# Dropping a kernel's closing barrier, and moving one small variance operation forward, in a linear-attention plus gated-MLP layer

## The chip, the cores and the metric

The kernel runs on one core of one Trainium2 chip. The metric is the device time of one execution in microseconds. The time is a little longer than the span of the profile, which runs from the kernel's first instruction to its last. In this text PE is TensorE, DVE is VectorE, ACT is ScalarE, POOL is GpSimd and SP is SyncE, as in the profile.

Ratios are the mean time of one kernel's fast runs over the mean of the other's fast runs of the same rounds, so they are not quite the ratio of the medians that are quoted beside them.

## The reference

The input has 2048 tokens of 640 columns. It is normalised, and the result goes through a linear attention with 32 heads of 20 and through a gated MLP of width 1536; both are added to the input.

```python
def _layernorm(x, axis=-1, eps=1e-5):
    m = jnp.mean(x, axis=axis, keepdims=True)
    v = jnp.var(x, axis=axis, keepdims=True)
    return (x - m) / jnp.sqrt(v + eps)
# ... (in reference():)
    xn = _layernorm(x, axis=-1)
    return x + _A_ref(xn, A_wqkv, A_w_phi, A_wo) + _B_ref(xn, B_w1, B_w3, B_w2)
```

## The kernel before

The kernel records all operations as Python objects, orders them with a list scheduler, and then plays one list of waits and operations into each engine. Tokens are worked on in 16 tiles of 128. What matters here is the head, in which the first tiles are normalised so that PE can start, and the tail.

Tile 0 is normalised by DVE statistics and a POOL power of -0.5. The sums of tile 1 are made by ACT; two small DVE operations turn them into mean square and variance, and POOL makes `rstd` of it, the factor 1 / sqrt(variance) by which normalisation multiplies (`mv` holds mean and variance, `bst` DVE's statistics, `x_tok` the tokens):

```python
    def act_rstd(t):
        v, r = mv[:, t, 1:2], rstd[:, t, 0:1]
        small(v, sums[:, 0:1], sums[:, 8:9], ALU.subtract)          # DVE, 1 column
        P.op("POOL", "tensor_tensor", [r], [v, mhalf[:, 0:1]], (r, v, mhalf[:, 0:1], ALU.pow), cost=0.6)

    def ln_apply(t, lo=0, hi=D):      # (x - mean) * rstd on DVE for the first four tiles
        ...
    def norms():
        ...
        yield lambda: act_sums(1)
        yield lambda: ln_stats(0, 1)
        yield lambda: ln_sums(2, 0)
        yield lambda: act_mean(1)
        yield lambda: ln_apply(0, 0, 256)
        done["first"] = 1
        yield lambda: ln_apply(0, 256, D)
        done["first"], done["ln"] = 2, 1
        yield lambda: act_rstd(1)
        yield lambda: (ln_sums(2, 1), ln_rstd(2, 1))
        yield lambda: ln_apply(1)
        done["ln"] = 2
        yield lambda: ln_apply(2)
        ...
```

PE transposes each normalised tile and multiplies it with the V weights, which arrive in three pieces:

```python
    def first_loads():
        load_x(0, 1)                                    # SP's queue
        o = P.dma("ACT", x_tok[:, 1:2, :], x_t[:, 1:2, :])
        ...
        load_x(2, 3)
        for a, b in ((0, 2), (2, 4), (4, DC)):          # V weights
            P.dma("SP", WVK[:, a:b, 0:D], wqkv_t[:, a:b, 2 * D:3 * D])
        load_x(3, 4)
        ...
```

At the end SP waits for all output stores. The lists are played inside a block, and the block closes with a branch, a drain and an all-engine barrier. In the instruction records each engine's drain raises a semaphore; POOL waits for it (the gather) and then raises a second one (the release), for which the other four wait (265.648 to 265.864 us in the kernel before; the records are listed below):

```python
        for o in finish:
            lists["SP"].append(("wait", o.sem[2], o.sem[1]))
    ...
    with nc.allow_low_precision(...), nc.allow_non_contiguous_dma(...), nc.Block() as block:

        @block.sync
        def _(e):
            play(lists["SP"], nc.sync)
        # ... the same for tensor, scalar, vector, gpsimd
```

The softmax here doesn't subtract the row's maximum and nothing guards it: scores larger than these inputs give would overflow.

## Time and profile before

| | us |
|---|---|
| time, median of the first 3 runs (267.52 to 267.91) | 267.78 |
| span of the profiled run, whose time was 267.64 | 265.864 |
| SP's wait for the last store ends | 265.431 |
| time minus span | 1.78 |

The table of stretches of the kernel before; the numbers behind the engines are busy microseconds, with instructions in brackets, then the granted clock of PE.

```profile
core 0: us, PE busy (x) PEld busy (x) DVE busy (x) ACT busy (x) POOL busy (x), PEclk, DMA share, GB/s
0.00:7.11 7.11, 5.67 (x24) 2.47 (x24) 3.63 (x13) 3.88 (x8) 3.40 (x15) 1.00 0.69 218
7.11:263.57 256.46, 256.44 (x1867) 153.40 (x1867) 179.93 (x299) 102.42 (x218) 92.51 (x93) 1.00 0.44 101
263.57:265.90 2.33, 0.00 (x0) 0.00 (x0) 0.29 (x1) 0.00 (x0) 0.00 (x0) 1.00 0.23 70
```

Between 7.11 and 263.57 us PE has no free time, so only the head and the tail can give anything back without less work for PE. The chain of waits of the kernel before (start, length, what) shows the head's steps:

```profile
4.57 0.58 POOL rstd L104
...
5.43 0.37 DVE x_tok L104
5.81 0.12 DVE mv L104
5.93 0.41 DVE bst L104
...
6.36 0.22 DVE mv L104
...
6.61 0.46 DVE x_tok L104
7.07 0.05 issue
7.11 256.46 PE PS L104 x1867
263.57 0.02 issue
263.60 0.29 DVE xres L104
```

From 5.17 on, the chain is DVE alone: both pieces of tile 0, the variance of tile 1 (`mv`, 5.81), statistics of tile 2 (`bst`, `mv`), then tile 1 (`x_tok`, 6.61). The timeline of DVE and of POOL in the same kernel has the durations that the change shifts:

```profile
5.72 0.21 DVE L104 TENSOR_SCALAR mv<-sums 128x1 f32<-128x1 f32 x1
5.85 0.48 DVE L104 BATCH_NORM_STATS2 bst<-x_tok 128x6 f32<-128x320 bf16 x1
6.36 0.22 DVE L104 BATCH_NORM_AGGREGATE mv<-bst 128x2 f32<-128x15 f32 x1
6.61 0.45 DVE L104 TENSOR_SCALAR x_tok<-x_tok,mv,rstd 128x640 bf16<-128x640 bf16 x1
7.25 0.45 DVE L104 TENSOR_SCALAR x_tok<-x_tok,mv,rstd 128x640 bf16<-128x640 bf16 x1 [0.19 <-POOL rstd L104]
...
6.01 1.20 POOL L104 TENSOR_TENSOR rstd<-mv,mhalf 128x1 f32<-128x1 f32 x2 [0.87 <-DVE mv L104]
```

POOL's two powers (tile 1 at 6.01, tile 2 at 6.665) took 0.565 and 0.549 us in the instruction records; the first ends just when DVE is through with the aggregation.

The tail, from the instruction records of the trace (start and end in us, sequencer instructions included):

```
263.597 263.889  DVE   last addition
264.249          SP    last store issued (end of the issue)
265.403 265.431  SP    wait for the last store
265.471 265.512  SP    compare-and-branch
265.648 265.655  SP    drain
265.681 265.698  POOL  gather     265.759 265.776  POOL  release
265.801 265.864  SP, ACT, DVE, PE: wait for the release
```

### The profile page before, as it was taken

The page shows a single profiled execution, that of the slowest core. Times are in us where ns is not written, and L with a number is a line of the kernel's source. Part 1 is how long each engine was busy: PE and PEld are TensorE (multiplying, and loading weights), DVE is VectorE, ACT ScalarE, POOL GpSimd, SP SyncE. Part 2 cuts the span into 40 slices and gives each one's busy share as a digit, 9 for nine tenths or more (in the row PEclk, how much of TensorE's full clock was granted, in tenths as well). Part 3 has the DMA queues.
Part 4 walks back from the last instruction along what each step waited for, and adds up shares of the span by engine and source line. Part 5 has one row for each costly group of instructions (what it writes and reads, how often), then busy time and mean ns, then how long its engine had stood idle before and what let it go on. Part 6 is the DMA issues. An engine that isn't in the chain of part 4 may idle for free.

```text
span 265.9 us, 4695 instructions
## 1 busy us (share of the span) xinstructions
PE 262.1 (99%) x1891; PEld 155.9 (59%) x1891; DVE 183.9 (69%) x313; ACT 106.3 (40%) x226; POOL 95.9 (36%) x107
## 2 busy tenths in 40 slices
PE   7999999999999999999999999999999999999996
PEld 3655545565558556465565756455656564777773
DVE  4668999999796679696685858788769567512112
ACT  5546988699760452251405240263143322000000
POOL 4221587989997035106030523007303321000000
DMA  6997088723301981932525070613260626141211
GB/s 211 270 307 205 8 161 242 162 52 55 117 2 22 270 195 39 140 56 62 94 49 128 2 159 25 131 25 75 62 133 22 132 52 128 27 123 52 87 39 49
DMA packets 62742, 27.73 MB, mean 104 GB/s; under 512 B 49920, under 2 KB 62720, under 8 KB 62720
## 3 DMA queue, kind: packets, MB, share of 16 engines
q1 hardware_dynamic: 62576, 27.26, 44.0%
q8 instruction: 15, 0.25, 0.4%
q10 hardware_dynamic: 144, 0.16, 0.2%
q14 instruction: 7, 0.06, 0.1%
HBM read 12.81 MB, written 2.62 MB: 58 GB/s over the span
## 4 chain that ended last, share of the span: by engine, by line
PE 96%; DVE 1%; DMA 1%; POOL 0%; issue 0%
PE PS L104 96%; DMA x_tok<-in_A_x_dram 1%; DVE bst L104 1%; DVE x_tok L104 0%; DVE mv L104 0%; POOL rstd L104 0%; DVE xres L104 0%
## 5 line engine op out<-in xcount | busy, mean ns | idle before, releaser
L104 PE MATMUL PS<-xnT,w_s 128*128 128x512 bf16 x480 | 108.2, 379 | 0.0
L104 PEld LDWEIGHTS PS<-xnT,w_s 128*128 128x128 bf16 x480 | 46.4, 98 | 50.9
L104 POOL TENSOR_TENSOR eqt<-eqt,rS 128x600 bf16<-128x600 bf16 (+1 forms) x32 | 41.0, 1306 | 97.4 <-DVE rS L104 97.4
L104 ACT ACTIVATE th<-PS 128x512 f32<-128x512 f32 x48 | 28.6, 596 | 79.0 <-PE PS L104 78.9
L104 PE MATMUL PS<-w_s,hT 128*128 128x320 bf16 (+2 forms) x384 | 54.9, 299 | 0.0
L104 DVE SCALAR_TENSOR_TENSOR t<-th,PS 128x512 bf16<-128x512 f32 x48 | 32.4, 675 | 31.4 <-ACT th L104 31.4
L104 PEld LDWEIGHTS PS<-w_s,hT 128*128 128x128 bf16 x384 | 37.1, 98 | 15.1
L104 PE MATMUL PS<-WVK,xnT 128*128 128x512 bf16 (+3 forms) x260 | 45.6, 330 | 0.1
L104 POOL TENSOR_TENSOR ekt<-ekt,rS 128x640 bf16<-128x640 bf16 x32 | 39.8, 1276 | 4.8 <-DVE rS L104 4.8
L104 ACT ACTIVATE eqt<-PS 128x240 bf16<-128x240 f32 (+1 forms) x96 | 27.2, 348 | 25.9 <-PE PS L104 24.1
L104 DVE TENSOR_TENSOR xres<-PS,xres 128x640 bf16<-128x640 f32 (+2 forms) x17 | 13.3, 782 | 33.5 <-PE PS L104 33.5
L104 PEld LDWEIGHTS PS<-WVK,xnT 128*128 128x128 bf16 x260 | 24.2, 98 | 19.4 <-ACT WVK L104 0.4
L104 DVE SCALAR_TENSOR_TENSOR hT<-t,PS 128x512 bf16<-128x512 bf16 x48 | 33.0, 687 | 1.7
L104 DVE TENSOR_REDUCE S<-ekt 128x64 f32<-128x1280 bf16 x16 | 23.3, 1455 | 2.2 <-ACT ekt L104 2.1
L104 PE MATMUL PS<-wo_s,oT 128*128 128x320 bf16 (+2 forms) x160 | 24.5, 299 | 0.0
L104 PE MATMUL PS<-Wqp,xnT 128*128 128x360 bf16 (+1 forms) x160 | 24.3, 299 | 0.0
L104 DVE TENSOR_REDUCE S<-eqt 128x66 f32<-128x1320 bf16 x16 | 24.2, 1510 | 0.0
L104 ACT ACTIVATE ekt<-PS 128x640 bf16<-128x640 f32 x32 | 22.3, 703 | 1.3 <-PE PS L104 0.8
L104 PEld LDWEIGHTS PS<-Wqp,xnT 128*128 128x128 bf16 x160 | 15.2, 98 | 7.6
L104 DVE RECIPROCAL rS<-S 128x64 f32<-128x64 f32 (+1 forms) x32 | 17.9, 560 | 1.1
L104 PEld LDWEIGHTS PS<-wo_s,oT 128*128 128x128 bf16 x160 | 15.2, 98 | 5.9
L104 DVE TENSOR_TENSOR o_tok<-PS,g_s 128x360 bf16<-128x360 f32 (+1 forms) x32 | 15.7, 491 | 1.1
(50 smaller groups left out, 124.3 us busy)
## 6 DMA issues: line engine op xcount, KB each, us to landing
w_s<-in_B_w_dram SPq DMA_DIRECT2D x6, 640.0 KB, 6.4
xres<-in_A_x_dram SPq DMA_DIRECT2D x16, 160.0 KB, 2.5
out_dram<-xres SPq DMA_DIRECT2D x15, 160.0 KB, 1.9
x_tok<-in_A_x_dram SPq DMA_DIRECT2D x3, 640.0 KB, 4.8
w_s<-in_B_w_dram SPq DMA_DIRECT2D x1, 1920.0 KB, 9.3
wo_s<-in_A_wo_dram SPq DMA_DIRECT2D x1, 800.0 KB, 4.8
WVK<-in_A_wqkv_dram SPq DMA_DIRECT2D x2, 320.0 KB, 4.5
x_tok<-in_A_x_dram SPq DMA_DIRECT2D x3, 160.0 KB, 2.7
```

What stands on the lines that cost most here:

```text
L104: o = _Op(eng, lambda: m(*args, **kw), r, w, cost)
```

## The change

Intent: give back the 0.43 us that the block's close takes after the last store, and let POOL start on tile 1's `rstd` earlier by placing the variance between the two pieces of tile 0's normalisation.

```diff
         yield lambda: ln_apply(0, 0, 256)
         done["first"] = 1
+        yield lambda: act_rstd(1)
         yield lambda: ln_apply(0, 256, D)
         done["first"], done["ln"] = 2, 1
-        yield lambda: act_rstd(1)
         yield lambda: (ln_sums(2, 1), ln_rstd(2, 1))
@@
-    with nc.allow_low_precision(...), nc.allow_non_contiguous_dma(...), nc.Block() as block:
-        @block.sync
-        def _(e):
-            play(lists["SP"], nc.sync)
-        (... and so for the four other engines)
+    with nc.allow_low_precision(...), nc.allow_non_contiguous_dma(...):
+        for e in ("SP", "PE", "ACT", "DVE", "POOL"):
+            play(lists[e], P.eng[e])
```

The programs differ in nothing else: no matmul, no load and no other wait changes place on any engine. The barrier at the kernel's entry stays.

More of the change, by code (lines that the diff above doesn't have):

```diff
@@ L933, in play @@
                     r.then_inc(it[2], it[3])
-    with nc.allow_low_precision(reason="bf16 results"), nc.allow_non_contiguous_dma(reason="w_phi rows"), nc.Block() as block:
-        @block.sync
-        def _(e):
-            play(lists["SP"], nc.sync)
-        @block.tensor
-        def _(e):
-            play(lists["PE"], nc.tensor)
-        @block.scalar
-        def _(e):
-            play(lists["ACT"], nc.scalar)
-        @block.vector
-        def _(e):
-            play(lists["DVE"], nc.vector)
-        @block.gpsimd
-        def _(e):
-            play(lists["POOL"], nc.gpsimd)
+    with nc.allow_low_precision(reason="bf16 results"), nc.allow_non_contiguous_dma(reason="w_phi rows"):
+        for e in ("SP", "PE", "ACT", "DVE", "POOL"):
+            play(lists[e], P.eng[e])
 _INS = ['A_x', 'A_wqkv', 'A_w_phi', 'A_wo', 'B_x', 'B_w1', 'B_w3', 'B_w2']
```

## The prediction

> **What bounds the kernel now.** TensorE does. In the table of stretches it is busy 256.44 of the 256.46 us between 7.11 and 263.57 us, at granted clock 1.00. The chain of waits is 7.1 us of head, 256.46 us of PE, 0.29 us of the last VectorE addition; then the output store lands and the kernel closes. Only head and tail are left, and the change touches exactly these.
>
> **Tail (no block).** From the trace's instruction records, sequencer instructions included: SP's wait for the last store ends at 265.431. Then come SP's branch (265.471 to 265.512), SP's drain (265.648), POOL's gather and release (265.681 to 265.776) and every engine's release wait, the last (PE) ending at 265.864, which is the span. The instruction order of the changed kernel has neither these drains nor this barrier; its last instruction is SP's wait. That removes 265.864 - 265.431 = 0.43 us, all on the critical path, as nothing runs beside it.
>
> The time (267.8) is longer than the span. [...] The trace's semaphore records agree: nine updates of one semaphore, 277.400 to 277.931 on the trace's clock, 0.24 to 0.77 us after the span's end. Its third step comes 0.21 us after the second; the same step in the next such barrier takes 0.04. So some engine comes late there. Without the closing barrier four engines reach it well before SP, so this 0.17 us may vanish from the time too. Estimate for the time: -0.43 to -0.65 us.
>
> At the start each engine loses a branch. The trace shows none of these (the only branch recorded is SP's last), and the entry barrier stays. I expect 0 to 0.05 us.
>
> **Head (variance of tile 1 earlier).** In the timeline VectorE does: first piece (5.173), second piece (5.434), the small variance operation (5.723, taking a slot of 0.124), half statistics of tile 2 (5.847), aggregation (6.364 to 6.586), tile 1's normalisation (6.610 to 7.057). The last waits for POOL's rstd, whose semaphore comes at 6.585. After: the variance at about 5.434, the second piece at 5.558, the statistics unchanged, rstd done 0.29 earlier. VectorE then flows from the aggregation into tile 1 with its usual overlap of 0.08, starting near 6.50: 0.1 us earlier, not 0.29, because VectorE itself is the next limit. PE idles 0.225 before tile 1's transposes, so these come about 0.1 earlier. Tile 0's second transposes come 0.12 later, but PE waits for ScalarE's first copy then (6.34), so that hides. Tile 2's rstd doesn't move (it waits for the aggregation), so PE will now wait about 0.04 for it: net 0.06 us gained, carried through the saturated PE stream to the end.
>
> **Sum.** Span -0.5 us, to 265.4; time -0.5 to -0.7 us: 267.2 us, range 266.8 to 267.6. Chances: faster by over 2% 0.005, within 2% 0.99, slower 0.005.
>
> **What would show each step right or wrong.** Tail: the last instruction is SP's store wait, about 1.54 us after the last addition ends (before 1.98). Runtime: time minus span shrinks from 1.78 to about 1.6 or stays. Head: tile 1's normalisation starts near 6.50 without a wait for POOL, its transposes near 7.00, and the long PE piece starts or ends 0.05 to 0.1 earlier while its length stays near 256.4.
>
> **What would make it wrong.** The runtime's barrier may cost the same or take over the wait, leaving the time gain near 0.1; the second piece's delay of 0.12 may reach PE through ScalarE's second copy (6.242 to 6.734), eating the head's gain; a chip other than the one of before may differ by more than the effect.

(The figures "277.400 to 277.931 on the trace's clock" are 266.103 to 266.634 us from the span's start. These nine updates are called the barrier after the kernel below. "The runtime's barrier" stays as a name only, since no trace shows whose updates they are. -0.43 for the block's close, 0 to -0.17 for the nine updates, 0 to -0.05 for the start and -0.06 for the head come to -0.5 to -0.7, so 267.2. The 0 to 0.05 is the author's estimate; the one branch recorded, SP's last, takes 0.041. The "usual overlap of 0.08" is in the trace before: the small variance operation ends at 5.930, the statistics after it start at 5.847.)

## The result

| | before | changed |
|---|---|---|
| time, median of 6 runs | 267.68 (267.52 to 268.33) | 266.97 (266.52 to 267.33) |
| ratio of the fast runs, 95% interval | | 0.9968 (0.9953 to 0.9984) |
| time of the profiled run | 267.64 | 266.57 |
| its span | 265.864 | 265.337 |

This is within 2%, and the median is inside the predicted range. The parts of the sum are not all as predicted. The profiled pair can be taken apart completely. Both traces end with two bursts of nine updates of semaphore 2, which no instruction of the kernel names; the second runs from 267.464 to 267.821 in the kernel before and from 266.405 to 266.761 in the changed one. The first burst is the barrier after the kernel; that its steps wait for the engines is shown below. The time is 0.18 to 0.19 us less than the very last update in both traces (267.821 and 267.64; 266.761 and 266.57), and 0.18 to 0.20 less in all fourteen traces. So the measured time moves with the last update, and what makes these bursts end earlier makes it shorter.

| from the traces, us | before | changed | difference |
|---|---|---|---|
| SP's wait for the last store ends | 265.431 | 265.337 | -0.094 |
| from there to the last instruction (branch, drain, barrier) | 0.433 | 0 | -0.433 |
| from there to the first burst complete (the barrier after the kernel) | 0.770 | 0.278 | -0.492 |
| from there to the last update of the second | 1.187 | 1.146 | -0.041 |
| sum | 267.821 | 266.761 | -1.060 |

The third row is the surprise, and it is larger than the block's own closing barrier. The nine updates of the barrier after the kernel, in us from the span's start:

```
before   266.103 266.137 266.348 266.393 266.416 266.513 266.552 266.588 266.634   (kernel ends 265.864)
changed  263.642 263.676 263.715 263.945 265.451 265.496 265.534 265.568 265.615   (kernel ends 265.337)
```

In the changed kernel four of the nine updates are done long before SP ends. The stretches and the chain of the changed kernel, against those shown of before:

```profile
7.11:263.57 256.46, 256.36 (x1867) 153.15 (x1865) 180.08 (x300) 102.36 (x218) 92.63 (x93) 1.00 0.45 102
263.57:265.90 2.33, 0.00 (x0) 0.00 (x0) 0.23 (x1) 0.00 (x0) 0.00 (x0) 1.00 0.23 70
```

```profile
4.58 0.58 POOL rstd L104
...
5.44 0.21 DVE mv L104
5.65 0.30 DVE x_tok L104
...
5.99 0.34 PE PS L104 x3
6.34 0.01 issue
6.35 257.13 PE PS L104 x1871
263.48 0.02 issue
263.50 0.29 DVE xres L104
```

The last addition starts 0.1 us earlier (263.50, before 263.60). DVE's chain now ends with tile 0's second piece, and PE's unbroken part starts already at 6.35. The timeline of DVE and POOL in the changed kernel:

```profile
5.44 0.21 DVE L104 TENSOR_SCALAR mv<-sums 128x1 f32<-128x1 f32 x1
5.57 0.37 DVE L104 TENSOR_SCALAR x_tok<-x_tok,mv,rstd 128x384 bf16<-128x384 bf16 x1
6.51 0.38 DVE L104 TENSOR_SCALAR x_tok<-x_tok,mv,rstd 128x640 bf16<-128x640 bf16 x1
7.34 0.45 DVE L104 TENSOR_SCALAR x_tok<-x_tok,mv,rstd 128x640 bf16<-128x640 bf16 x1 [0.44 <-POOL rstd L104]
...
5.73 0.63 POOL L104 TENSOR_TENSOR rstd<-mv,mhalf 128x1 f32<-128x1 f32 x1 [0.58 <-DVE mv L104]
6.68 0.63 POOL L104 TENSOR_TENSOR rstd<-mv,mhalf 128x1 f32<-128x1 f32 x1 [0.32 <-DVE mv L104]
```

Tile 1 is normalised at 6.51 without a wait for POOL, as predicted; but both powers now take 0.63, so that tile 2 starts at 7.34 and not at 7.25. PE's timeline in the kernel before and, in the second fence, in the changed one:

```profile
6.34 0.72 PE L104 MATMUL PS<-WVK,xnT 128*128 128x320 bf16 x4
7.11 0.45 PE L104 MATMUL PS<-ident,x_tok 128*128 128x128 bf16 x5
7.40 0.71 PE L104 MATMUL PS<-WVK,xnT 128*128 128x320 bf16 x4
```

```profile
6.35 0.72 PE L104 MATMUL PS<-WVK,xnT 128*128 128x320 bf16 x4
6.96 0.45 PE L104 MATMUL PS<-ident,x_tok 128*128 128x128 bf16 x5
7.24 0.71 PE L104 MATMUL PS<-WVK,xnT 128*128 128x320 bf16 x4
```

PE comes to the second piece of the V weights (the last line of each) 0.16 us earlier; after tile 2's wait 0.09 of it is left at the end.

### The profile page after: what moved, and what is told of

Same layout as the page of the kernel before. It is cut to its first block, busy times and chain, and to the rows that moved or that the text cites. A ratio compares the mean times of both kernels' runs of the same rounds, so it can differ in the third digit from the quotient of the medians.

```text
span 265.3 us, 4684 instructions
## 1 busy us (share of the span) xinstructions
PE 262.1 (99%) x1891; PEld 155.8 (59%) x1891; DVE 183.8 (69%) x313; ACT 106.3 (40%) x226; POOL 96.1 (36%) x107
## 4 chain that ended last, share of the span: by engine, by line
PE 97%; DMA 1%; DVE 1%; POOL 0%; issue 0%
PE PS L104 97%; DMA x_tok<-in_A_x_dram 1%; DVE bst L104 0%; POOL rstd L104 0%; DVE mv L104 0%; DVE x_tok L104 0%; DVE xres L104 0%
## 5 line engine op out<-in xcount | busy, mean ns | idle before, releaser
L104 POOL TENSOR_TENSOR eqt<-eqt,rS 128x600 bf16<-128x600 bf16 (+1 forms) x32 | 41.1, 1307 | 97.3 <-DVE rS L104 97.3
```

The source lines that it names most:

```text
L104: o = _Op(eng, lambda: m(*args, **kw), r, w, cost)
```

## The experiments

Twelve further kernels ran, two of them the changed kernel again, all with correct results. The first four ran on one chip with 11 runs of the kernel before (median 267.71, 267.55 to 269.58), then four on a second chip, then four on a third with 11 runs of before (median 267.75, 267.35 to 268.32). Five rounds give 6 runs of each kernel.

| kernel | mean (lowest to highest) | time minus span, mean (range) | ratio to before, 95% interval |
|---|---|---|---|
| changed, first | 266.93 (266.52 to 267.33) | 1.25 (1.22 to 1.30) | 0.9968 (0.9953 to 0.9984) |
| no_block_only | 266.89 (266.61 to 267.13) | 1.22 (1.21 to 1.24) | 0.9960 (0.9940 to 0.9981) |
| variance_only | 267.95 (267.46 to 268.26) | 1.75 (1.71 to 1.78) | 1.0000 (0.9978 to 1.0021) |
| changed_again | 266.97 (266.49 to 267.64) | 1.25 (1.21 to 1.29) | 0.9963 (0.9939 to 0.9987) |
| barrier_back | 267.52 (267.27 to 267.73) | 1.73 (1.67 to 1.76) | 0.9986 (0.9964 to 1.0008) |
| v_weights_sooner | 267.55 (267.02 to 268.82) | 1.23 (1.19 to 1.27) | 0.9988 (0.9968 to 1.0008) |
| v_sooner_old_variance | 268.31 (267.15 to 269.93) | 1.24 (1.21 to 1.27) | 1.0016 (0.9986 to 1.0047) |
| changed_third | 266.84 (266.49 to 267.15) | 1.24 (1.19 to 1.27) | 0.9960 (0.9946 to 0.9974) |
| v_weights_later | 268.68 (267.22 to 269.61) | 1.23 (1.19 to 1.31) | 1.0031 (1.0001 to 1.0060) |

(Spans of single runs are listed to 0.1 us, so a single difference is good to about 0.05.) The 22 runs of before have a time minus span of 1.68 to 1.81. So this difference goes with a kernel's close, and the spread between runs of one kernel (0.46 to 2.78 us in this table) lies inside the span.

### Each half of the change alone

`no_block_only` is the changed kernel with the variance in its old place; `variance_only` is the kernel before with only the variance moved; `changed_again` is the changed kernel once more.

```diff
 no_block_only, against the changed kernel:
-        yield lambda: act_rstd(1)
         yield lambda: ln_apply(0, 256, D)
         done["first"], done["ln"] = 2, 1
+        yield lambda: act_rstd(1)

 variance_only, against the kernel before: the reverse of this, the block stays
```

> Only the block is removed; the variance keeps its old place. Theory (the time gain is the tail: 0.43 us of closing barrier plus about 0.49 us by which the runtime's own barrier after the kernel gets shorter; the head gives only 0.09): time 0.9 us below before (about 266.9), trace: last store's wait ends near 265.43 as before, the span ends with it, tile 1's normalisation starts near 6.61 as before, time minus span near 1.23. Rival A (the runtime's barrier costs the same, so the tail is worth only 0.43 and the rest is the head or drift between runs): about 267.3, time minus span near 1.78. Rival B (the head's reordering gives most): 267.5 or more.

> Only the variance is moved; the block stays. Theory: trace as in the changed kernel at the head (tile 1's normalisation near 6.51, tile 2's near 7.34, long PE part ends about 0.09 us earlier), tail as before (last store's wait to span's end 0.43, time minus span 1.78): time 0.1 us below before, which repeats can't tell from zero. Rival B (the head gives most of the 0.85 us): 0.5 us or more below before, clear of the interval.

> The changed kernel again, beside the others on one chip. Theory: 266.9 us, ratio 0.9965 to 0.997, head and tail as in its first trace; the single runs spread over 0.8 us as before, with time minus span near 1.23 in each, so that the spread lies within the span. Rival C (its first trace was a lucky fast run): a trace whose span is 265.8 or more, with a longer stretch somewhere that shows what the spread is.

Taking the block away alone gives all of the time that can be measured: its mean is 0.90 below the nine runs of before that stay under 269 us (mean 267.79; two runs were at 269.5), against 0.92 from the two rows of the tail (0.433 + 0.492), and time minus span is 1.22. (With the two runs at 269.5 in, the mean of before is 268.11 and the difference 1.22; their time minus span is as in the others, so they are long within the span. No trace shows why.) Its trace has the last store's wait end at 265.375 with the span, tile 1 at 6.564 and the barrier after the kernel complete 0.272 later. That decides against rival A (267.3, 1.78) and rival B.

Moving the variance alone shows nothing in the time (ratio 1.0000). Its trace has the head as in the changed kernel (tile 1 at 6.438, tile 2 at 7.263) and the tail as before (0.438 and 0.769). But the end of PE's work did not come 0.09 earlier: it came at 264.149, and in the trace of `changed_again` at 264.535, 1.07 later than in the changed kernel's first trace. That trace is the one that rival C named, with a span of 266.4. So the question was what makes a span longer by up to 1 us with the very same instructions.

The waits of `changed_again` between 5 and 10 us (engine, line, waited for: us in total, times, longest) answer it:

```profile
DVE bst L104 <- DMA x_tok<-in_A_x_dram: 1.3, 1, 1.3
PEld PS L104 <- ACT xnT L104: 1.3, 2, 1.0
PE PS L104 <- DMA WVK<-in_A_wqkv_dram: 0.9, 1, 0.9
```

PE waits for the second piece of the V weights. (The second line is the same wait, put down to the semaphore that the profile saw last: ACT's copies were over by 8.05.) Landing of that piece, PE's start on it, and end of PE's work, in all traces but that of `v_weights_later`, which comes below, in us:

```
                       landed   PE starts   PE ends   ends - starts
before                 7.039    7.404       263.559   256.16
changed                6.927    7.244       263.465   256.22
no_block_only          7.120    7.357       263.512   256.16
variance_only          7.727    7.863       264.149   256.29
changed_again          8.160    8.295       264.535   256.24
barrier_back           7.060    7.206       263.427   256.22
last_wait_on_pe        6.980    7.152       263.373   256.22
last_wait_on_dve       6.851    7.241       263.502   256.26
last_wait_on_pool      7.476    7.612       263.827   256.22
last_wait_on_act       7.075    7.448       263.605   256.16
changed_third          7.503    7.638       263.909   256.27
v_weights_sooner       6.523    7.695       263.917   256.22
v_sooner_old_variance  7.189    7.987       264.141   256.15
```

From its start on this piece PE needs 256.15 to 256.29 us in each of these traces. Where the piece lands at 7.47 or later, PE starts 0.135 to 0.136 after the landing, in all four such traces. So in the traces with the same order of loads the spans differ mainly through one load. (There is a second, smaller source: in `last_wait_on_act` the clock record has full clock only from 6.84 us on, the first matmuls on the V weights are 0.24 and 0.22 us apart instead of 0.136, and PE reached the second piece at 7.448 though it had landed at 7.075.) Of the load queue's packets that end between 3.5 and 8.5 us, the median one takes 0.055 us, but in `changed_again` 19 of 1257 take over 0.3 and the longest 1.54. The landing semaphore of a piece is raised in sixteen steps, and the table has the last of them: in `changed_again` fifteen steps were in by 7.105 and the sixteenth came at 8.160, where in the first trace of the changed kernel they end at 6.867 and 6.927. So one late step out of sixteen held PE up. That trace too has 17 of 1307 packets over 0.3 (longest 1.05), so their number does not tell the two apart. What makes single packets slow is not shown, nor which of them delayed that step.

### The barrier put back without the block

```diff
         for e in ("SP", "PE", "ACT", "DVE", "POOL"):
             play(lists[e], P.eng[e])
+        nc.all_engine_barrier()
```

> The changed kernel with one explicit all-engine barrier at its end: no block, no branches, but the barrier is back. Theory: the barrier alone is the cost. After SP's last wait some 0.25 to 0.30 us of drain, gather and release follow (0.43 before, less SP's branch and the 0.14 us after it), and the runtime's barrier becomes as long as before (time minus span 1.78): time 267.6 to 267.7, at most 0.25 below before. Rival D (the branches, or the block's placing of the instructions, were the cost): stays near 266.9.

In the trace, 0.265 us of drain, gather and release follow SP's last wait (265.290 to 265.555), and the barrier after the kernel again needs 0.769 from the end; time minus span is back at 1.73. The mean is 0.55 above `changed_again` on the same chip. The trace's parts, 0.265 + 0.49 = 0.76, would have it at 0.76; the runs' spread (0.46 and 1.15 us from lowest to highest) is wide enough for the difference. Rival D (the time stays near 266.9) falls: the barrier is most of the cost, 0.76 of the 0.92. Of the 0.433 us before, the other 0.17 went with SP's branch and the time until the drain behind it.

### Which engine ends last

Another engine than SP waits for the output stores:

```diff
         for o in finish:
-            lists["SP"].append(("wait", o.sem[2], o.sem[1]))
+            lists["PE"].append(("wait", o.sem[2], o.sem[1]))      # or DVE, POOL, ACT
```

> The changed kernel, but TensorE instead of SP waits for the output stores, so TensorE is the last engine to end. Theory (the engines reach the runtime's barrier one after another in a fixed order, with TensorE first and SP at the turn, so an engine that ends early takes its step early and only the steps from the last engine on remain): from the end of the last wait to the barrier's ninth update 0.55 to 0.62 us, against 0.278 with SP last; all nine updates come after that end. Rival (the barrier just starts later; which engine ends last makes no difference): 0.28 as with SP.

> The same with VectorE waiting for the stores. Theory (VectorE takes the fourth step: in the changed kernel the fourth update came 0.15 us after VectorE's last addition): three updates come long before the end, six after it, and the ninth 0.38 to 0.45 us after the last wait's end. Rival: 0.28.

> The same with POOL waiting for the stores. Theory (POOL takes the third step, and is the engine that came 0.17 us late in the kernel before): two updates before the end, the third 0.5 to 0.6 us after it, the ninth 0.8 to 0.9 us after it, the worst place of the five. Rival 1 (POOL takes the second step, ScalarE was the late one): one update before the end, the ninth about 0.6 us after it. Rival 2 (no order): 0.28.

> The same with ScalarE waiting for the stores. Theory (ScalarE takes the second step): one update before the end, the ninth 0.5 to 0.6 us after it. Rival (ScalarE is third and late): two updates before the end, the ninth 0.8 us or more after it.

Measured, from the end of the last wait, which is the span's end:

| waits last | updates before the end | end to its own first update | end to the ninth update |
|---|---|---|---|
| PE | 0 | 0.187 | 0.542 |
| ACT | 1 | 0.110 | 0.434 |
| POOL | 2 | 0.532 | 0.814 |
| DVE | 3 | 0.141 | 0.383 |
| SP (changed kernel) | 4 | 0.114 | 0.278 |
| all at once (kernel before) | 0 | 0.24 (PE's) | 0.770 |

Each place is one trace, but the counts are as the theory has them in all four: PE, ACT, POOL, DVE, SP take the steps of the barrier after the kernel in this order. The sizes were a little below what was expected for PE (0.55 to 0.62) and ACT (0.5 to 0.6), and within it for DVE and POOL. POOL alone comes 0.53 us after its last instruction, the others 0.11 to 0.19. This explains the row of before: the closing barrier lets all engines go at once, POOL's release ends at 265.776, and the third update comes 0.572 later, at 266.348; six more steps follow. Without the closing barrier POOL has taken its step by 263.715. So the 0.49 us are the steps of four engines, and above all POOL's, done while the last store was still on its way. Why POOL needs 0.53 is open.

### The V weights' landing moved, both ways

The orders of all compute engines stay exactly as in the changed kernel; only one load changes its place in a queue after the schedule is made.

```diff
 v_weights_sooner: the load of token tile 2 moves from SP's list to ACT's, behind that of tile 1
+    for it in [it for it in lists["SP"] if it[0] == "op" and it[1] is moved[-1]]:
+        lists["SP"].remove(it)
+        at = next(n for n, i in enumerate(lists["ACT"]) if i[0] == "op") + 1
+        lists["ACT"].insert(at, it)
 v_sooner_old_variance: the same, on no_block_only
 changed_third: no edit
 v_weights_later: the load of token tile 3 moves ahead of the V weights in SP's list
+    lists["SP"].insert(2, lists["SP"].pop(5))
```

> The changed kernel; only the load of token tile 2 is issued by ScalarE's queue behind that of tile 1 instead of by SP, so that SP issues the three pieces of the V weights 0.45 us sooner. Every compute engine's order is unchanged. Theory (the spread of 0.8 us between runs of one kernel is the landing of the second V piece, 6.93 to 8.16 us in the traces so far, for which TensorE waits from 7.2 on): the second piece lands near 6.5 in a good run, TensorE starts on it near 7.2 in nearly every run, the spread falls below 0.5 us and the mean to 266.5 to 266.8, below the changed kernel's 266.95. Rival E (the spread comes from elsewhere, for instance the end): spread and mean as in the changed kernel. Risk: tile 2 or tile 0 lands later and delays VectorE's first normalisation beyond 5.3 us; then the mean gets no better.

> The same, but with the variance in its old place. Theory (the variance move is worth 0.10 us where the V weights don't limit): the long TensorE part ends 258.39 us after the start of the first normalisation, against 258.28 with the move, and the mean is 0.1 us above the run before this one, which five rounds will hardly tell from zero. Rival (the move is worth nothing on the chip, the 0.10 in the traces being the weights' luck): 258.28 in both.

> The changed kernel for the third time, as the baseline of this call: mean near 266.95, spread near 0.8 us; single runs that differ do so within the span, time minus span staying near 1.23. Its trace has the long TensorE part ending 256.2 us after the start on the second V piece, whenever that piece lands.

> The changed kernel; only the load of token tile 3 (160 KB) is issued ahead of the V weights instead of behind them. Theory (the second V piece's landing sets the head): 160 KB at the 300 to 380 GB/s of this stretch, plus 0.43 us of SP's issue, put the landings 0.4 to 0.6 us later, beyond what TensorE can hide: it starts on the second piece at 7.5 to 7.8 in a good run, mean 0.3 to 0.5 us above the changed kernel, 267.2 to 267.5. Rival E: no change.

`v_weights_sooner` landed the second piece at 6.523, as expected, and was no better (mean 267.55), because its stated risk came true: tile 2 landed at 5.094 instead of 4.021. DVE's list has half of tile 2's statistics before tile 0's normalisation, and so DVE stood still; its timeline:

```profile
5.12 0.49 DVE L104 BATCH_NORM_STATS2 bst<-x_tok 128x6 f32<-128x320 bf16 x1 [0.65 <-DMA x_tok<-in_A_x_dram]
5.53 0.20 DVE L104 TENSOR_SCALAR sums<-mv 128x1 f32<-128x1 f32 x1
5.64 0.34 DVE L104 TENSOR_SCALAR x_tok<-x_tok,mv,rstd 128x256 bf16<-128x256 bf16 x1
```

Tile 0 is normalised 0.46 later than in the changed kernel, and PE ends 0.45 later. The spread did not fall (1.8 us, where under 0.5 was expected), so this run doesn't confirm the theory of the landing as hoped. In its trace another load had become the limit; what spread its other runs is not shown.

With its partner it does settle the variance. From the start of the first normalisation to the end of PE's work, where the V weights don't hold PE up:

```
variance moved:        changed 258.283   barrier_back 258.282   last_wait_on_pe 258.284   v_weights_sooner 258.275
variance in old place: before  258.386   no_block_only 258.386  v_sooner_old_variance 258.374
```

The move is worth 0.10 us, repeated to 0.01 (`last_wait_on_dve` lost 0.08 of it again in the fold of the key weights, with a gap of 0.09 at 17.1 us). The rival, which had the same number in both, falls. It does not show in the times: `no_block_only` and `changed_again` differ by 0.08 the wrong way, and `v_sooner_old_variance` is 0.76 above its partner, with two runs (269.13 and 269.93) whose listed granted clock is 0.994.

`changed_third` came out as expected (mean 266.84, PE's 256.27 from the second piece on).

`v_weights_later` gave its expected 267.2 to 267.5 in two runs (267.22 and 267.39), and something else in four: 269.17 to 269.61. The listed granted clock is 1.0 in the two and 0.994 in the four. The profiled run is one of the four; its stretches:

```profile
6.00:7.00 1.00, 0.22 (x3) 0.04 (x1) 0.75 (x3) 0.67 (x2) 0.68 (x2) 1.00 0.92 311
7.00:8.00 1.00, 0.56 (x3) 0.40 (x4) 0.78 (x2) 0.00 (x0) 0.19 (x1) 0.80 0.97 341
8.00:9.00 1.00, 1.00 (x9) 0.81 (x7) 0.79 (x3) 0.20 (x1) 0.07 (x1) 0.50 1.08 383
9.00:10.00 1.00, 1.00 (x6) 0.54 (x5) 0.00 (x0) 0.61 (x2) 0.48 (x1) 0.50 1.10 369
10.00:11.00 1.00, 1.00 (x8) 0.78 (x7) 0.00 (x0) 0.60 (x2) 0.00 (x0) 0.50 1.15 305
11.00:12.00 1.00, 1.00 (x9) 0.72 (x8) 0.10 (x1) 0.87 (x3) 0.00 (x0) 1.00 1.76 175
```

The chain of waits of the same run shows what PE waited for first:

```profile
2.19 5.11 DMA WVK<-in_A_wqkv_dram
7.31 0.14 issue
7.44 8.09 PE PS L104 x55
```

The first piece landed at 7.31, PE had a gap of 1.22 us before 7.44, and for 3.41 us, from 7.59 to 11.01, the granted clock was half (0.50, the column before the DMA share). Before the fall PE was busy until 4.87, in two bursts of 0.29 and 0.34 us after 5.47, and from 7.44 on. Which of this made the clock fall, and what brought it back, is not shown. In this trace the landings were later than expected: 7.307 for the first piece (5.86 to 6.72 in the eleven traces with the changed kernel's order of loads) and 8.143 for the second (6.85 to 8.16). So the kernel with the later landing was slower, and most of that lies in the four runs that list the lower clock (mean 269.37, against 267.31 for the two at 1.0); those two were slower by the expected amount, but have no trace. Rival E (no change) falls. That the landing also makes the spread of the runs without a trace is not shown.

None of the twelve beats the changed kernel; `no_block_only` equals it in time.

## Why the prediction was right or wrong

- **The kernel's own close, -0.43.** Right: 0.433 in the traces, and 265.337 - 263.795 = 1.54 us from the last addition to the end, as stated. `barrier_back` shows that the barrier is 0.265 of it.
- **The barrier after the kernel, 0 to -0.17 (time minus span to about 1.6, or unchanged).** That it gets shorter when four engines end early was right, the size was wrong. It measured -0.49 (0.770 to 0.278), and time minus span fell from 1.74 to 1.24 (means). The prediction took only the one late step of 0.17 from the records. It did not ask which steps of the nine an engine that ends early can take in advance: the cost follows the last engine's place in the order and its own delay: 0.81 with POOL last, against 0.28 with SP last in the changed kernel.
- **The start, 0 to -0.05.** Nothing: the first matmul starts at 1.05 in both kernels.
- **Tile 1's normalisation near 6.50 without a wait, its transposes near 7.00.** Right: 6.515 and 6.95.
- **"Tile 2's rstd doesn't move."** Wrong: its normalisation came at 7.339 instead of 7.250, because POOL's power took 0.627 instead of 0.549. In all eleven traces with the variance moved both powers take 0.625 to 0.631, in the three without it 0.548 to 0.565. Why is open. Both longer powers start while DVE is inside a normalisation (5.730 in 5.566 to 5.937, 6.677 in 6.515 to 6.898); but so does tile 2's power before (6.665, inside 6.610 to 7.057), and that took 0.549. No run here shows what makes the power longer.
- **"Net 0.06 us gained" at the head.** Too small: 0.10. The prediction had PE wait about 0.04 for tile 2. That fits if it took the weight load of tile 2's transposes (7.813) for the start of their matmuls; it does not say so. Before the change PE only reached these 0.13 later, at 7.947, so there was more to gain: PE came 0.16 earlier to the second V piece just before. POOL's slower power took part of it back. That the sum came near is partly luck: the two errors have opposite signs.
- **The sum.** Predicted 267.2; median 266.97. The barrier after the kernel gave 0.32 us more than the largest value of its term, which more than covers the difference. The spread between the six runs of the changed kernel is 0.8 us and larger than any of the errors. In its three traces it comes from the landing of the V weights (PE starts on the second piece at 7.244, 7.638 and 8.295, and ends at 263.465, 263.909 and 264.535); the prediction had named only the chip as a source of such scatter (the medians of before on the two chips with 11 runs are 267.71 and 267.75).

## What to carry to other kernels

The barrier at the end of this kernel was paid twice: 0.27 us itself, and 0.49 us because it set all engines free at the same moment for the nine updates that come next. Where a kernel's trace shows the same, let each engine end as soon as its work is done, and leave the wait for the last store to the engine that leaves least of these updates to come, here SP (0.28 us) and not POOL (0.81 us). Moving the small operation forward helped by the distance to the next limit only, 0.10 of the 0.29 us by which its result came earlier. An effect of this size is read between two fixed points of several traces, since here the landing of one load spread the end of PE's work by 1.07 us over three traces of the same kernel.
